# First pair's k and q through SyncE's queue in fp32, cast on VectorE; half of the first q split on GpSimd

## The chip, the cores and the metric

The kernel runs on one core of one Trainium2 chip. The metric is the device time of one execution, in microseconds; the median of the runs counts. The core has a matrix engine (TensorE, PE in the profile), VectorE (DVE), ScalarE (ACT), GpSimd (POOL) and SyncE (SP). Each has its own instruction queue and works through it in order; semaphores order them among each other. DMAs are issued from a queue: here GpSimd issues all loads, since its DMAs can cast fp32 to bf16 on the way, and SyncE issues the stores of the output.

## The reference

Sparse attention and, on its output, a soft mixture of experts. Inputs are q, k and v of shape (4, 8, 768, 64): 4 batches, 8 heads, 768 positions, 64 channels.

```python
k_min, k_max = k_chunks.min(axis=3), k_chunks.max(axis=3)      # 24 chunks of 32 keys
ub = np.sum(np.maximum(q * k_min, q * k_max), axis=-1)         # upper bound per query and chunk
ub = np.where(causal, ub, -1e9)
top_chunks = np.argsort(ub, axis=-1)[..., -6:]                 # six chunks for each query
scores = np.where(sel & causal_by_position, q @ k.T / 8, -1e9)
attn = softmax(scores) @ v
# x: attention output as (3072, 512)
logits = x @ phi                                               # 32 slots, 4 for each of 8 experts
slot_input = softmax(logits, axis=0).T @ x
slot_out[e] = relu(slot_input[e] @ w1[e]) @ w2[e]
out = softmax(logits, axis=1) @ slot_out
```

## The kernel before

The work is cut into 16 pairs of heads (4 for each batch). The two heads of a pair share the 128 partitions: 64 channels of one head above 64 of the other.

For a pair, k and q are loaded with 128 partitions of six positions each, TensorE transposes them in 12 small matmuls a tensor (`transposes`, L233), and ScalarE copies the result out of PSUM as kT and qT (`evac_T`, L242). VectorE takes the minimum and the maximum of each chunk of kT (`kmin` L251, `kmax` L257) and spreads them into a block-diagonal tile bd (L259). q is split into a negative part, min(q, 0), and a positive part, max(q, 0) (`qsplit`, L267 to L271; the positive part of the first pair is a ReLU on ScalarE, L269). Then the upper bound is the negative part times k_min plus the positive part times k_max: 12 matmuls (`ubound`, L284), on top of a causal bias (L277). VectorE finds the eight largest per query (L296) and marks the chunks below the sixth (`select`, L299); GpSimd adds one column (L298). These marks are transposed (L307, L315) and added into the score matmuls through a mask matrix smask (L325 and L335). ScalarE takes exponentials (L349), GpSimd zeroes the diagonal blocks above the diagonal (L359), TensorE multiplies with v (L377).

The order is written by hand: the engines run in the order of the program text. Before the loop stands a prologue (L170 to L616) which starts pair 0, prepares pairs 1 and 2, and fills TensorE's waits with matmuls on constants (`warm`, L224). The loop body (L618 to L720) interleaves pair i's scores with the bounds of pair i + 1, the transposes of pair i + 2 and the products with v of pair i - 1, and weaves in the expert work of a finished batch. After the loop come the experts and the output: the weights w1 and w2 of 8 experts are loaded during the whole loop, one 1 MB tile after another (`load_w`, L144), 14 into tiles of their own that are reserved from the start (w_sb), the last expert's w2 in four quarters (w_last, L150), which are used last (`last_expert_out`, L921). Output rows of 256 x 512 leave through SyncE's queue (L969, L990, L992).

At the start GpSimd issues, in this order: k and q of pair 0, k of pair 1, the select that makes the identity matrix ident (L175), q of pair 1, k and q of pairs 2 and 3, v of pair 0, four selects for the constants qgrp, caus and squad (L195 to L207), and the first weight (L211). Then comes the copy that fills the first half of smask (L213), which needs schunk from VectorE (L572).

The prologue's lines around the change:

```python
warm(8)
transposes(0, "k")
evac_T(0, "k")
kmin(0)
kmax(0)
warm(2)
transposes(0, "q")
evac_T(0, "q")
qsplit(0)
```

Of the kernel before, what the change touches and what calls it, by code (L numbers as in the profile page):

```python
# [9 lines left out]
F32 = mybir.dt.float32  # L10
# [9 lines left out]
NQT = 6  # L20
# [39 lines left out]
def kernel(  # L60
# [75 lines left out]
    def load_w(i):  # L136

        if i < E:
            src = moe_w1[i].rearrange("(a p x) f -> p a (x f)", p=P, x=2)
            dst = w_sb[i].rearrange("p (a f) -> p a f", a=NDG // 2)  # L140
        else:
            src = moe_w2[LATE[i - E]].rearrange("(a p x) d -> p a (x d)", p=P, x=4)
            dst = w_sb[i].rearrange("p (a f) -> p a f", a=NFG // 4)
        nc.gpsimd.dma_start(out=dst, in_=src)  # L144
# [8 lines left out]
    def load(i, nm, n=1):  # L153

        b, j = divmod(i, NPB)
        t = ring[nm][i // 2 % 2][:, 2 * (i % 2):2 * (i % 2 + n)]
        src = {"k": k, "q": q}[nm][b, 2 * j:2 * (j + n)]
        nc.gpsimd.dma_start(out=t, in_=src.rearrange("h (p g) d -> p h (g d)", p=P))
        for x in range(n):
            st[nm, i + x] = t[:, 2 * x:2 * x + 2]  # L160

    def load_v(i):
# [6 lines left out]

    nc.vector.memset(ones_sq, 1.0)  # L170
    nc.vector.memset(ident, 0.0)
    load(0, "k")
    load(0, "q")
    load(1, "k")
    nc.gpsimd.affine_select(  # L175
        out=ident, in_=ident, compare_op=ALU.not_equal, fill=1.0, base=0,
        pattern=[[-1, P]], channel_multiplier=1,
    )
    for t in (squad, caus, qgrp, headsel, ns_t[0], ns_t[1], c_pad):
        nc.vector.memset(t, 0.0)  # L180
    for t in v_t:
# [26 lines left out]
        out=squad, in_=squad, compare_op=ALU.not_equal, fill=-1.0, base=-NCHUNK,  # L208
        pattern=[[-CH, 2], [-64, 2], [0, NCHUNK]], channel_multiplier=1,
    )  # L210
    load_w(0)  # L211
    def spread_mask(t0, t1, copy):
        copy(  # L213
            smask[:, :, t0:t1].rearrange("p o t a x -> p o (t a) x"),
# [5 lines left out]
    def warm(n):  # L220
        r = ones_sq.rearrange("p (o c) -> p o c", o=1).broadcast_to([P, 4, P])
        for _ in range(n):
            for x in range(2):
                nc.tensor.matmul(  # L224
                    warm_ps[:, 2 * x:2 * x + 2], lhsT=ones_sq, rhs=r[:, :2], start=True, stop=True)
# [38 lines left out]
    def qsplit(i):  # L264
        qT = st["qT", i]
        t = tpu.tile([P, 2, S], BF16, name="qpn", tag="qpn")
        nc.vector.tensor_scalar_min(t[:, 0, :], qT, 0.0)  # L267
        if i == 0:
            nc.scalar.activation(t[:, 1, :], qT, func=ACT.Relu)  # L269
        else:  # L270
            nc.vector.tensor_scalar_max(t[:, 1, :], qT, 0.0)  # L271
        st["qpn", i] = t
# [45 lines left out]
    def scores(i, g):  # L318
        ps = p_sc.tile([P, 2, 512], F32, name="sc_ps", tag="sc")
        kT, qT, nsT = st["kT", i], st["qT", i], st["nsT", i]  # L320
        for kg, q0, w, c in (GROUPS_LAST if i == LAST else GROUPS)[g]:
            qs = slice(kg * P + q0, kg * P + q0 + w)
            for h in range(2):
                r = slice(h * 64, (h + 1) * 64)
                nc.tensor.matmul(  # L325
                    ps[:, h, c:c + w], lhsT=kT[r, kg * P:(kg + 1) * P], rhs=qT[r, qs],
                    start=True, stop=False,
                )
            t0, t1 = kg + q0 // P, kg + (q0 + w) // P
            runs = [(x, max(t0, x * NJ), min(t1, (x + 1) * NJ)) for x in range(2)]  # L330
            runs = [r for r in runs if r[1] < r[2]]
            for x, f, l in runs:
                for h in range(2):
                    r = slice(h * 64, (h + 1) * 64)
                    nc.tensor.matmul(  # L335
                        ps[:, h, c + (f - t0) * P:c + (l - t0) * P],
                        lhsT=smask[r, x, kg].rearrange("p a b -> p (a b)"),
                        rhs=nsT[r, (f - x * NJ) * P:(l - x * NJ) * P], start=False, stop=(l == t1),
                    )
        st["scps", i, g] = ps  # L340

    def expo(i, g, masked=True):
        pieces = (GROUPS_LAST if i == LAST else GROUPS)[g]
        w = sum(x[2] for x in pieces)
        if w == 512:
            e = ep.tile([P, 2, 512], BF16, name="e_sb", tag="e_sb")
        else:
            e = ep3.tile([P, 2, 384], BF16, name="e3_sb", tag="e3_sb")
        nc.scalar.activation(e[:, :, :w], st.pop(("scps", i, g))[:, :, :w], func=ACT.Exp, scale=scale)  # L349

        st["e", i, g] = e
        if masked:
            mask(i, g)
# [187 lines left out]
    def moe_ct_copy(b):  # L541
        nc.vector.tensor_copy(cT_all[:, b * NQT:(b + 1) * NQT, :], st.pop(("ctps", b)))


    def have(i):
        return 0 <= i < NPAIR

    def moe(step, i):

        if have(i) and i % NPB == NPB - 1:  # L550
            step(i // NPB)
# [5 lines left out]
    def weights(i):  # L557
        nonlocal nw
        for _ in range(wplan.get(i, 0)):
            load_w(nw)  # L560
            nw += 1

    warm(8)
    transposes(0, "k")
    evac_T(0, "k")
# [3 lines left out]
    transposes(0, "q")  # L569
    evac_T(0, "q")  # L570
    qsplit(0)
    nc.vector.tensor_tensor(schunk[:, :, :, 0], squad[:, :, 0, :], squad[:, :, 1, :], op=ALU.add)  # L572
    spread_mask(0, NJ, nc.gpsimd.tensor_copy)
    warm(2)
# [40 lines left out]
    kmax(2)  # L615
    qsplit(2)  # L616

    for i in range(1, NPAIR):  # L618
        slots = have(i - 3) and (i - 3) % NPB == NPB - 1
        if i >= EARLY:  # L620
            wt = ctx.enter_context(tc.tile_pool(name=f"wt{i}", bufs=1))
            if i < LAST:
                w_sb.append(wt.tile([P, NFG * Dm], BF16, name=f"w_sb{i}"))
                weights(i)
            else:
                w_last = [wt.tile([P, NFG, Dm // 2], BF16, name=f"w_last{y}") for y in range(2)]
                for y in (1, 0):
                    load_w_half(w_last[y], y)
        scores(i, 0)
        expo(i, 0)  # L630
        moe(moe_max, i - 3)
        scores(i, 1)
        expo(i, 1)
        if have(i + 1):
            ubound(i + 1)
        if i < LAST - 1:
            moe(moe_bound, i - 3)
        if have(i - 2):
            normalise(i - 2)
        if i == LAST - 1:  # L640
            moe(moe_bound, i - 3)
        if i == LAST:
            moe_ct_copy(B - 2)
        if have(i + 1):
            select(i + 1)
        moe(moe_comb, i - 3)
        if have(i + 2):
            transposes(i + 2, "k")
            evac_T(i + 2, "k")
        if not slots:  # L650
            if have(i + 2):
                load_v(i + 2)
            if i < EARLY:
                weights(i)
        if i != LAST - 1:
            pv(i - 1, [0, 1, 2])
        for g in (2, 3):
            scores(i, g)
            expo(i, g, not slots)
            if g == 2 and i == LAST - 1:  # L660
                pv(i - 1, [0, 1, 2])
            if g == 2 and i == LAST:
                x_transposes(i - 2)
        moe(moe_exp, i - 3)
        if slots:
            mask(i, 2)
            mask(i, 3)
        if have(i - 2) and i < LAST:
            x_transposes(i - 2)
        pv(i - 1, [3])  # L670
        if have(i + 2):
            transposes(i + 2, "q")
            evac_T(i + 2, "q")
            kmin(i + 2)
        if i < LAST - 1:
            moe(moe_exp2, i - 3)
        if have(i - 2):
            evac_x(i - 2)
        if have(i + 2):
            kmax(i + 2)  # L680
        if i < LAST - 1:
            moe(moe_scale, i - 3)
        if slots:
            if have(i + 2):
                load_v(i + 2)
            if i < EARLY:
                weights(i)
        scores(i, 4)
        expo(i, 4)
        if have(i + 5) and i % 2:  # L690
            load(i + 5, "k", 2)
            load(i + 5, "q", 2)
        if i == LAST - 1:
            moe(moe_exp2, i - 3)
            moe(moe_scale, i - 3)
        if i == LAST:
            pv(i - 1, [4, 5])
        moe(moe_comb2, i - 3)
        scores(i, 5)
        expo(i, 5)  # L700
        if have(i + 1):
            ns_transposes(i + 1)
            evac_ns(i + 1)
        if i < LAST:
            pv(i - 1, [4])
        moe(moe_dispatch, i - 3)
        if i < LAST:
            pv(i - 1, [5])
        if have(i + 2):
            qsplit(i + 2)  # L710
        if i < LAST - 1:
            moe(moe_ct, i - 4)
        elif i == LAST - 1:
            moe(moe_ct, i - 3)
        moe(moe_logits, i - 2)
        moe(moe_copy, i - 2)
        if i == LAST - 2:
            l_ctx.close()
        if i == LAST - 1:
            u_ctx.close()  # L720
# [304 lines left out]
```

## Time and profile before

| | |
|---|---|
| median of three runs | 159.91 us (158.8 to 159.99) |
| span of the profiled execution, first to last instruction | 156.8 us |
| its own time, taken as its span and what lies around it | 3.1 us between that span and the median |
| TensorE busy | 136.5 us (87%) |
| VectorE, ScalarE busy | 121.9 and 122.8 us (78% each) |
| GpSimd busy | 98.7 us (63%) |
| moved by GpSimd's DMA queue | 26.25 MB in 40032 packets |
| moved by the other queue, the stores | 6.29 MB in 3072 packets |
| mean granted TensorE clock | 0.982 of full speed |

The profile gives one execution. Rows of a timeline hold the start and the duration in microseconds, the engine, the line, the operation, the tile written and the tiles read, shapes, the count, and in brackets how long the engine had been idle before and what released it. PEld is a weight load of TensorE. In a window's row stand the length, then the busy time and count of PE, PEld, DVE, ACT and POOL, the granted clock, the DMA share and GB/s. Bytes are counted where they are written, so a load that casts to bf16 counts half of what it reads.

### The profile page before, as it was taken

To read this page: it belongs to the slowest core of one execution; us is meant where nothing else is said; L and a number is where in the kernel's file an instruction comes from. 1 tells how busy PE (TensorE), PEld (TensorE's weight loads), DVE (VectorE), ACT (ScalarE), POOL (GpSimd) and SP (SyncE) were. 2 spreads that over 40 slices of the span, in tenths; PEclk is the share of its full clock that TensorE was granted. 3 is DMA by queue.
4 is the path that set the end of the run, shared out by engine and by line. 5 is a ranking of instruction groups with operands and counts; after the bars stand their busy time and mean duration, and the time that the engine had idled before them with its cause. 6 is when DMAs were issued, how large, how long until landed. Compare 5 with 4: busy or idle time off the path is not lost.

```text
span 156.8 us, 5988 instructions
## 1 busy us (share of the span) xinstructions
PE 136.5 (87%) x2464; PEld 93.2 (59%) x2464; DVE 121.9 (78%) x437; ACT 122.8 (78%) x171; POOL 98.7 (63%) x192
## 2 busy tenths in 40 slices
PE   7796789999999999999999899999979999977500
PEld 4463466767766776766777677766657854633100
DVE  5478887999999998999899899999753761178720
ACT  3479899999999889999989999998789532276520
POOL 6999647958877876697597975869696810000000
PEclk9999999999999999999999999999999999999975
DMA  2999999999999999999999999999999999949995
GB/s 37 160 172 195 194 193 221 172 201 203 196 214 199 201 202 207 204 197 210 186 198 205 205 203 201 208 200 198 211 197 216 212 215 198 151 158 399 419 420 223
DMA packets 43131, 32.92 MB, mean 210 GB/s; under 512 B 26208, under 2 KB 37984, under 8 KB 43104
## 3 DMA queue, kind: packets, MB, share of 16 engines
q0 software_dynamic: 40032, 26.25, 113.9%
q1 hardware_dynamic: 3072, 6.29, 10.3%
q8 instruction: 19, 0.31, 0.7%
q14 instruction: 8, 0.07, 0.1%
HBM read 52.49 MB, written 6.29 MB: 375 GB/s over the span
## 4 chain that ended last, share of the span: by engine, by line
PE 54%; ACT 18%; DVE 12%; issue 6%; DMA 5%; POOL 1%; DVEq 0%; ACTq 0%; POOLq 0%
ACT e_sb L349 11%; PE sc_ps L325 10%; PE at_ps L377 8%; PE sc_ps L335 7%; PE tr_ps L233 5%; PE xT_ps L399 4%; ACT qT L242 4%; DMA out_dram<-o_sb 3%; DMA q_in<-in_q_dram 3%; PE ub_ps L284 2%; PE h_ps L852 2%; PE ub_ps L277 2%; DVE x_sb L390 2%; DVE o_sb L944 1%; DVE mx L296 1%
## 5 line engine op out<-in xcount | busy, mean ns | idle before, releaser
L349 ACT ACTIVATE e_sb<-sc_ps 128x1024 bf16<-128x1024 f32 (+1 forms) x96 | 83.2, 919 | 6.0 <-PE sc_ps L335 5.5
L359 POOL TENSOR_SCALAR_AFFINE_SELECT e_sb<-e_sb 128x256 bf16<-128x256 bf16 x96 | 40.2, 437 | 17.6 <-ACT e_sb L349 17.4
L325 PE MATMUL sc_ps<-qT,kT 64*128 64x384 bf16 (+3 forms) x258 | 36.8, 306 | 2.9 <-ACT e_sb L349 2.2
L335 PE MATMUL sc_ps<-nsT,smask 64*128 64x384 bf16 (+2 forms) x294 | 38.1, 284 | 0.1
L377 PE MATMUL at_ps<-v_t,e_sb 128*128 128x65 bf16 x642 | 27.7, 193 | 0.9 <-PE sc_ps L335 0.6
L377 PEld LDWEIGHTS <-e_sb 128*128 128x128 bf16 x642 | 23.6, 97 | 3.5 <-issue 1.3
L325 PEld LDWEIGHTS <-kT 64*128 64x128 bf16 x258 | 14.0, 93 | 10.9 <-issue 5.5
L296 DVE MAX8 mx<-ub_ps 128x8 f32<-128x8 f32 (+1 forms) x192 | 16.8, 162 | 3.2 <-PE ub_ps L284 3.0
L164 POOL DMA_DIRECT2D v_t<-in_v_dram x16 | 16.7, 1044 | 3.6 <-PE xT_ps L399 1.8
L251 DVE TENSOR_REDUCE mm<-kT 128x24 bf16<-128x768 bf16 x16 | 15.1, 944 | 3.0 <-ACT kT L242 2.9
L335 PEld LDWEIGHTS <-smask 64*128 64x128 bf16 x294 | 15.0, 94 | 3.6 <-issue 0.6
L390 DVE TENSOR_TENSOR x_sb<-at_ps,inv 128x768 bf16<-128x768 f32 (+1 forms) x17 | 15.5, 910 | 0.6
L242 ACT COPY kT<-tr_ps 128x768 bf16<-128x768 bf16 x16 | 12.9, 804 | 3.5 <-PE tr_ps L233 3.5
L257 DVE TENSOR_REDUCE mm<-kT 128x24 bf16<-128x768 bf16 x16 | 15.1, 943 | 0.0
L242 ACT COPY qT<-tr_ps 128x768 bf16<-128x768 bf16 x16 | 12.8, 801 | 2.4 <-PE tr_ps L233 2.4
L144 POOL DMA_DIRECT2D w_sb<-in_moe_w_dram x15 | 10.7, 712 | 0.0
L410 DVE COPY xT_sb<-xT_ps 128x768 bf16<-128x768 bf16 (+1 forms) x15 | 8.0, 536 | 1.6 <-PE xT_ps L399 1.6
L233 PE MATMUL tr_ps<-ident,q_in 128*64 128x128 bf16 x192 | 8.4, 223 | 0.7 <-DMA q_in<-in_q_dram 0.5
L233 PE MATMUL tr_ps<-ident,k_in 128*64 128x128 bf16 x192 | 8.4, 223 | 0.5 <-DMA k_in<-in_k_dram 0.5
L399 PE MATMUL xT_ps<-ident,x_sb 128*128 128x128 bf16 x96 | 8.3, 221 | 0.4 <-DVE x_sb L390 0.3
L271 DVE TENSOR_SCALAR qpn<-qT 128x768 bf16<-128x768 bf16 x15 | 8.3, 553 | 0.0
L284 PE MATMUL ub_ps<-bd,qpn 128*128 128x48 bf16 x192 | 7.6, 183 | 0.4 <-DVE qpn L267 0.4
(147 smaller groups left out, 209.7 us busy)
## 6 DMA issues: line engine op xcount, KB each, us to landing
w_sb<-in_moe_w_dram POOLq DMA_DIRECT2D x15, 1024.0 KB, 16.3
out_dram<-o_sb SPq DMA_DIRECT2D x8, 512.0 KB, 4.6
v_t<-in_v_dram POOLq DMA_DIRECT2D x16, 192.0 KB, 12.4
k_in<-in_k_dram POOLq DMA_DIRECT2D x7, 384.0 KB, 11.8
q_in<-in_q_dram POOLq DMA_DIRECT2D x7, 384.0 KB, 13.0
out_dram<-o_sb SPq DMA_DIRECT2D x8, 256.0 KB, 2.9
w_last<-in_moe_w_dram POOLq DMA_DIRECT2D x4, 256.0 KB, 19.6
k_in<-in_k_dram POOLq DMA_DIRECT2D x2, 192.0 KB, 4.1
```

The lines of the kernel that those rows point to most:

```text
L164: nc.gpsimd.dma_start(out=v_t[i % NV][:, :, :, :D], in_=v[b, 2 * j:2 * j + 2].rearrange("h (g p) d -> p h g d", p=P),)
L233: nc.tensor.matmul(ps[h * 64:(h + 1) * 64, g, :], lhsT=src[:, h, g * D:(g + 1) * D], rhs=ident, is_transpose=True,)
L242: nc.scalar.copy(t.rearrange("d (p g) -> d p g", g=NQT), st.pop((nm + "ps", i)).rearrange("d g p -> d p g"),)
L251: nc.vector.tensor_reduce(mm[:, 0, 0, :], kT, axis=AX.X, op=ALU.min)
L257: nc.vector.tensor_reduce(mm[:, 1, 0, :], kT, axis=AX.X, op=ALU.max)
L296: nc.vector.max(mx[:, a, :], ub[:, a, :max(8, 4 * t + 4)])
L325: nc.tensor.matmul(ps[:, h, c:c + w], lhsT=kT[r, kg * P:(kg + 1) * P], rhs=qT[r, qs], start=True, stop=False,)
L335: nc.tensor.matmul(ps[:, h, c + (f - t0) * P:c + (l - t0) * P], lhsT=smask[r, x, kg].rearrange("p a b -> p (a b)"), rhs=nsT[r, (f - x * NJ ...
L349: nc.scalar.activation(e[:, :, :w], st.pop(("scps", i, g))[:, :, :w], func=ACT.Exp, scale=scale)
L359: nc.gpsimd.affine_select(out=e[:, :, c:c + P], in_=e[:, :, c:c + P], compare_op=ALU.is_ge, fill=0.0, base=0, pattern=[[0, 2], [1, P]], ch ...
L377: nc.tensor.matmul(o, lhsT=st["e", i, g][:, h, c:c + P], rhs=v_t[i % NV][:, h, kg, :D + 1], start=(kg == 0), stop=(kg == t),)
L390: nc.vector.tensor_tensor(st["x", b][:, t0:t1, 2 * j:2 * j + 2, :].rearrange("p t h d -> p h t d"), at[:, :, :, :D], inv.broadcast_to([P, ...
```

## The change

The first pair's k and q are no longer loaded by GpSimd's casting DMA. SyncE issues two plain fp32 loads into a staging area, which lies in the tile of the fourteenth weight; that tile is loaded much later. VectorE casts the two into the ring buffers in which the other pairs arrive. On GpSimd, ident now comes ahead of the load of pair 1's k. The negative part of the first q moves from VectorE to GpSimd, and the first weight is asked for behind it. The loop body is rewritten: the calls of each iteration are named in four lists (for usual iterations, for those with expert work, for the last but one and the last), which a function `step` turns into calls.

```diff
-    load(0, "k")
-    load(0, "q")
-    load(1, "k")
+    stage = w_sb[EARLY - 1].bitcast(F32).rearrange("p (n h c) -> p n h c", n=2, c=512)[:, :, :, :NQT * D]
+    for n, (nm, src) in enumerate((("k", k), ("q", q))):
+        nc.sync.dma_start(out=stage[:, n], in_=src[0, :2].rearrange("h (p g) d -> p h (g d)", p=P))
     nc.gpsimd.affine_select(
         out=ident, in_=ident, compare_op=ALU.not_equal, fill=1.0, base=0,
         pattern=[[-1, P]], channel_multiplier=1,
     )
+    load(1, "k")
...
-    load_w(0)
...
-        nc.vector.tensor_scalar_min(t[:, 0, :], qT, 0.0)
+        (nc.gpsimd if i == 0 else nc.vector).tensor_scalar_min(t[:, 0, :], qT, 0.0)
...
+    def cast(n, nm):
+        t = ring[nm][0][:, :2]
+        nc.vector.tensor_copy(t, stage[:, n])
+        st[nm, 0] = t
+
+    cast(0, "k")
+    cast(1, "q")
     warm(8)
     transposes(0, "k")
...
     qsplit(0)
+    load_w(0)
     nc.vector.tensor_tensor(schunk[:, :, :, 0], squad[:, :, 0, :], squad[:, :, 1, :], op=ALU.add)
     spread_mask(0, NJ, nc.gpsimd.tensor_copy)
...
+    PLAIN = """sc:0 ex:0 mk:0 sc:1 ex:1 mk:1 ub norm sel trk evk lv lw pv:0:1:2 sc:2 ex:2 mk:2 sc:3 ex:3 mk:3
+        xt pv:3 trq evq kmin evx kmax sc:4 ex:4 mk:4 lkq sc:5 ex:5 mk:5 ns evns pv:4 pv:5 qs
+        moe_ct moe_logits moe_copy"""
...
+        order = FINAL if i == LAST else BEFORE_LAST if i == LAST - 1 else SLOTS if slots else PLAIN
+        for what in order.split():
...
+            step(i, what)
```

More of the change, by code (lines that the diff above doesn't have):

```diff
@@ L616, with step @@
     qsplit(2)
+    def step(i, what):
+        name, *arg = what.split(":")
+        arg = [int(x) for x in arg]
+        if name == "sc":
+            scores(i, arg[0])
+        elif name == "ex":
+            expo(i, arg[0], False)
+        elif name == "mk":
+            mask(i, arg[0])
+        elif name == "pv":
+            pv(i - 1, arg)
+        elif name == "norm":
+            if have(i - 2):
+                normalise(i - 2)
+        elif name == "xt":
+            if have(i - 2):
+                x_transposes(i - 2)
+        elif name == "evx":
+            if have(i - 2):
+                evac_x(i - 2)
+        elif name in ("ub", "sel", "ns", "evns"):
+            if have(i + 1):
+                {"ub": ubound, "sel": select, "ns": ns_transposes, "evns": evac_ns}[name](i + 1)
+        elif name in ("trk", "trq"):
+            if have(i + 2):
+                transposes(i + 2, name[2])
+        elif name in ("evk", "evq"):
+            if have(i + 2):
+                evac_T(i + 2, name[2])
+        elif name in ("kmin", "kmax", "qs"):
+            if have(i + 2):
+                {"kmin": kmin, "kmax": kmax, "qs": qsplit}[name](i + 2)
+        elif name == "lv":
+            if have(i + 2):
+                load_v(i + 2)
+        elif name == "lw":
+            if i < EARLY:
+                weights(i)
+        elif name == "lkq":
+            if have(i + 5) and i % 2:
+                load(i + 5, "k", 2)
+                load(i + 5, "q", 2)
+        else:
+            off = {"moe_dispatch": 3, "moe_ct": 4, "moe_logits": 2, "moe_copy": 2, "moe_ct3": 3}.get(name, 3)
+            fn = {
+                "moe_max": moe_max, "moe_bound": moe_bound, "moe_comb": moe_comb, "moe_exp": moe_exp,
+                "moe_exp2": moe_exp2, "moe_scale": moe_scale, "moe_comb2": moe_comb2, "moe_dispatch": moe_dispatch,
+                "moe_ct": moe_ct, "moe_ct3": moe_ct, "moe_logits": moe_logits, "moe_copy": moe_copy,
+                "moe_ctc": moe_ct_copy,
+            }[name]
+            moe(fn, i - off)
@@ new lines @@
+    PLAIN = """sc:0 ex:0 mk:0 sc:1 ex:1 mk:1 ub norm sel trk evk lv lw pv:0:1:2 sc:2 ex:2 mk:2 sc:3 ex:3 mk:3
+        xt pv:3 trq evq kmin evx kmax sc:4 ex:4 mk:4 lkq sc:5 ex:5 mk:5 ns evns pv:4 pv:5 qs
+        moe_ct moe_logits moe_copy"""
+    SLOTS = """sc:0 ex:0 mk:0 moe_max sc:1 ex:1 mk:1 ub moe_bound norm sel moe_comb trk evk pv:0:1:2 sc:2 ex:2 sc:3 ex:3
+        moe_exp mk:2 mk:3 xt pv:3 trq evq kmin moe_exp2 evx kmax moe_scale lv lw sc:4 ex:4 mk:4 lkq moe_comb2
+        sc:5 ex:5 mk:5 ns evns pv:4 moe_dispatch pv:5 qs moe_ct moe_logits moe_copy"""
@@ L618 @@
+    BEFORE_LAST = """sc:0 ex:0 mk:0 moe_max sc:1 ex:1 mk:1 ub norm moe_bound sel moe_comb trk evk sc:2 ex:2 pv:0:1:2
+        sc:3 ex:3 moe_exp mk:2 mk:3 xt pv:3 trq evq kmin evx kmax lv lw sc:4 ex:4 mk:4 lkq moe_exp2 moe_scale moe_comb2
+        sc:5 ex:5 mk:5 ns evns pv:4 moe_dispatch pv:5 qs moe_ct3 moe_logits moe_copy"""
+    FINAL = """sc:0 ex:0 mk:0 sc:1 ex:1 mk:1 norm pv:0:1:2 sc:2 ex:2 mk:2 xt sc:3 ex:3 mk:3
+        pv:3 evx sc:4 ex:4 mk:4 pv:4:5 sc:5 ex:5 mk:5"""
     for i in range(1, NPAIR):
@@ L628 @@
                     load_w_half(w_last[y], y)
[L629 to L716, printed above, removed]
+        order = FINAL if i == LAST else BEFORE_LAST if i == LAST - 1 else SLOTS if slots else PLAIN
@@ L717 @@
+        for what in order.split():
+            if i == LAST and what == "norm":
+                normalise(i - 2)
+                moe_ct_copy(B - 2)
+                continue
+            step(i, what)
         if i == LAST - 2:
```

## The prediction

> **What bounds the kernel now.** I read the page first, for the shares and the DMA rows, then the timeline of the first 13 us, where the change lies, then the timeline of the last 20 us, to see what a gain there would still meet.
>
> ```profile
> span 156.8 us, 5988 instructions
> ...
> DMA  2999999999999999999999999999999999949995
> ...
> q0 software_dynamic: 40032, 26.25, 113.9%
> ```
>
> No engine is the bound over the whole span, but the DMA engines are busy in nearly every slice, and nearly all of it is GpSimd's queue (q0), which casts fp32 to bf16 on the way.
>
> ```profile
> 3.00:4.00 1.00, 1.00 (x7) 0.71 (x5) 0.23 (x3) 0.00 (x0) 0.91 (x3) 1.00 1.10 145
> 4.00:5.00 1.00, 0.74 (x10) 0.32 (x10) 0.00 (x0) 0.00 (x0) 1.00 (x2) 1.00 1.26 177
> 5.00:6.00 1.00, 0.92 (x16) 0.52 (x12) 0.00 (x0) 0.58 (x1) 1.00 (x2) 1.00 1.11 111
> ...
> 137.00:138.00 1.00, 0.84 (x12) 0.41 (x9) 0.68 (x2) 0.87 (x3) 0.00 (x0) 1.00 0.42 65
> 138.00:139.00 1.00, 0.57 (x6) 0.31 (x6) 0.36 (x2) 0.27 (x1) 0.00 (x0) 1.00 0.01 1
> ```
>
> These are one-microsecond windows; the last column is GB/s. The queue starts to move bytes at about 3 us and runs dry at 138 us. In between it is one long backlog.
>
> ```profile
> 137.55 0.29 PE L921 MATMUL so_last<-w_last,hT_pad 128*32 128x256 bf16 x4
> 138.43 0.29 PE L921 MATMUL so_last<-w_last,hT_pad 128*32 128x256 bf16 x4 [0.58 <-DMA w_last<-in_moe_w_dram]
> 138.83 0.48 DVE L974 SCALAR_TENSOR_TENSOR so_all<-so_last,zinv,so_part 128x256 bf16<-128x256 f32 x1 [0.64 <-ACT o_sb L941]
> ```
>
> The end of that backlog is the last quarter of w_last, and TensorE waits for it. Without data missing, the second four L921 would have begun at 137.55 + 0.29 = 137.84 and not 138.43: compute has 0.59 us of slack there, and L974, from which most of the output hangs, follows. So the end is set by **two trains that arrive nearly together**: the compute chain from the first k and q, and the stream of GpSimd's queue. The time falls by the smaller of what the stream gains and what compute gains plus 0.59.
>
> Now the start, where both trains set off:
>
> ```profile
> 1.13 3.46 PE L224 MATMUL warm_ps<-ones_sq 128*128 128x256 bf16 x16 [1.13 <-DVE ones_sq L170]
> 1.32 0.84 POOL L158 DMA_DIRECT2D k_in<-in_k_dram  x1 [0.80 <-POOLq L1009]
> 2.15 0.73 POOL L158 DMA_DIRECT2D q_in<-in_q_dram  x1
> 2.87 0.72 POOL L158 DMA_DIRECT2D k_in<-in_k_dram  x1
> 3.69 0.31 POOL L175 TENSOR_SCALAR_AFFINE_SELECT ident<-ident 128x128 bf16<-128x128 bf16 x1
> 4.85 0.53 PE L233 MATMUL tr_ps<-ident,k_in 128*64 128x128 bf16 x12 [0.26 <-DMA k_in<-in_k_dram]
> 5.42 0.80 ACT L242 COPY kT<-tr_ps 128x768 bf16<-128x768 bf16 x1 [3.33 <-PE tr_ps L233]
> 6.25 0.95 DVE L251 TENSOR_REDUCE mm<-kT 128x24 bf16<-128x768 bf16 x1 [2.91 <-ACT kT L242]
> 6.40 0.53 PE L233 MATMUL tr_ps<-ident,q_in 128*64 128x128 bf16 x12 [0.48 <-DMA q_in<-in_q_dram]
> 6.96 0.80 ACT L242 COPY qT<-tr_ps 128x768 bf16<-128x768 bf16 x1 [0.75 <-PE tr_ps L233]
> 7.79 0.84 ACT L269 ACTIVATE qpn<-qT 128x768 bf16<-128x768 bf16 x1
> 8.10 0.26 DVE L259 TENSOR_TENSOR bd<-mm,headsel 128x96 bf16<-128x96 bf16 x1
> 8.27 0.35 DVE L267 TENSOR_SCALAR qpn<-qT 128x768 bf16<-128x768 bf16 x1
> 8.30 0.47 POOL L207 TENSOR_SCALAR_AFFINE_SELECT squad<-squad 128x96 bf16<-128x96 bf16 x1
> 8.70 0.46 PE L284 MATMUL ub_ps<-bd,qpn 128*128 128x48 bf16 x12
> 9.47 0.84 POOL L213 COPY smask<-schunk 128x768 bf16<-128x768 bf16 x1
> 12.15 4.37 ACT L349 ACTIVATE e_sb<-sc_ps 128x1024 bf16<-128x1024 f32 x5 [0.68 <-PE sc_ps L335]
> ```
>
> k lands at 4.85, q at 6.40. The upper bounds (L284, 8.70) wait for bd (8.10 + 0.26) and then for the negative half of q, L267, which stands behind it on VectorE. The first exponential comes at 12.15, and from there the loop runs with its engines full.
>
> **The change, part by part.** First, the loads on SyncE's queue. The trace has no fp32 load there; its nearest rows are the wait that starts SyncE's queue (total, times, longest) and its stores, 256 KB each in L969 and 512 KB in L992 (issue times, then landing times).
>
> ```profile
> SPq L1009 <- PEq L1009: 0.8, 1, 0.8
> ...
> L969 SPq DMA_DIRECT2D out_dram<-o_sb x6: 534/578/628, 138.0 to 141.8; - x6
> DMA to landing us min/median/max: 2.5/2.9/2.9
> ...
> L992 SPq DMA_DIRECT2D out_dram<-o_sb x8: 333/662/1120, 142.4 to 149.3; - x8
> DMA to landing us min/median/max: 3.4/4.6/5.3
> ```
>
> SyncE is free at 0.8 us. A 256 KB store landed in 2.5 us at best and a 512 KB one in 3.4; 384 KB lies half way, 2.95, so k lands near 3.8 (bounds 3.4 and, by the slowest store, 6.1). q is issued 0.6 later; the distance of the two stores makes 0.9 us for 256 KB more, 1.35 for 384 KB, so q lands near 5.2 (4.4 to 7.4).
>
> Second, two casts on VectorE, 768 fp32 elements a partition. Not in the trace; the bounds are 0.35 us (L267, bf16 to bf16) and 0.95 (L251, the same element count at one element a step). I take the middle, 0.65. They stand ahead of kmin, so **kmin also waits for q's landing**, and behind VectorE's opening memsets, which end long before 3.8.
>
> k: cast until 4.5, but TensorE has its 16 warm-up matmuls until 1.13 + 3.46 = 4.59, so the transposes begin at 4.6, 0.25 earlier than now. kT is there at 5.97, kmin starts at 6.0. q: cast 5.2 to 5.85, transposes 5.9 (0.5 earlier), qT done at 7.3, ReLU on ScalarE until 8.13. bd ends at 8.1 (0.25 earlier).
>
> Third, the negative half on GpSimd. GpSimd works without a break from 1.32 to 8.77, and two issues of 0.84 and 0.73 leave it, so its selects end at 8.77 - 1.57 = 7.2 and it is free when qT comes. The operation is not in the trace: the copy L213 of the same 768 elements took 0.84, VectorE's form 0.35, and GpSimd's two-input form gives the upper end:
>
> ```profile
> L460 POOL TENSOR_TENSOR ld<-lg,m_run 128x192 f32<-128x192 f32 x3 | 1.8, 597 | 0.0
> ```
>
> 597 ns for 192 elements is 3.1 ns each, 2.4 us for 768. I take the copy's 0.84, one input as here: 7.3 to 8.15. Behind the min on GpSimd wait the issue of the first weight and the mask copy (then 8.9 to 9.7, still ahead of 9.47 + 0.84 = 10.3 now), so moving the weight costs nothing: v and four loads stand ahead of it in the backlog. L284 can begin at about 8.2 instead of 8.70; bd, ReLU and min arrive within 0.05 us of each other. **Compute gains 0.5**, of which I keep 0.45, since behind the bounds TensorE also waits for the second pair's kT (ScalarE, 0.4 earlier).
>
> Fourth, the stream. k and q (192 KB each after the cast) leave it: by the windows they are gone at about 5.5 us (145 + 177 + half of 111, plus a little before 3 us, makes 393 KB). Afterwards the engines move 786 KB in fp32 for the same two, but from about 1 us earlier, and the second pair's k is issued behind ident alone, at 1.32 + 0.31 = 1.63 instead of 2.87. With q's last byte written half a microsecond before it lands (4.7), what follows starts 0.8 us earlier. I take **0.9 for the stream**, bounds 0 and 1.4.
>
> Fifth, the loop is rewritten as lists of steps. Read slot by slot they issue the same calls in the same order as the old body, the two last pairs included, so this costs nothing.
>
> The sum: the smaller of 0.9 and 0.45 + 0.59 = 1.04 is 0.9 at L974. Output stores of the first half-tiles move by 0.45 only, but the engines are nearly idle then (1 GB/s from 138 to 139), so I let only 0.1 be lost: 0.8 us. Span 156.8 to 156.0; the median of the runs, 159.91, lies 3.1 above the span, so **159.1 us**.
>
> **Where the Trainium skill speaks against it.** The trace shows VectorE's fast form beside GpSimd's DMA issues:
>
> ```profile
> 13.34 0.76 POOL L158 DMA_DIRECT2D q_in<-in_q_dram  x1
> 13.68 0.60 DVE L267 TENSOR_SCALAR qpn<-qT 128x768 bf16<-128x768 bf16 x1
> 14.07 0.73 POOL L144 DMA_DIRECT2D w_sb<-in_moe_w_dram  x1
> 14.20 0.78 DVE L271 TENSOR_SCALAR qpn<-qT 128x768 bf16<-128x768 bf16 x1
> ```
>
> The issues took their usual 0.73 to 0.76, and the operation that takes 0.35 at 8.27 took 0.60 and 0.78: here VectorE was held up. The Trainium skill ("SBUF — State Buffer", section "Who interferes with whom") says that a copy or cast in a two-port mode and GpSimd exclude each other for a whole instruction, whichever began first; its warning on "DVE blocks DMA" names the fp32 copy as one that keeps GpSimd from writing descriptors. By that rule GpSimd would lose the casts' time. The trace agrees that they collide, and shows so far the other loser.
>
> **The rivals.**
>
> 1. *The stream does not move.* The two loads use the same 16 engines whichever queue holds them, so what is saved in one queue is spent in the other and the end of w_last stays at 138.4. For: the DMA row is full everywhere. Against: the engines move almost nothing before 3 us. Then compute only waits longer: 0 to 0.2, 159.8 us. The Trainium skill ("DMA: Bandwidth & Descriptors", "Issuing engines are not separate DMA queues") states just this.
> 2. *The casts hold GpSimd.* Both casts fall into GpSimd's issues. If it waits out 2 x 0.65 us, its selects end at 8.5, min at 9.35, L284 starts 0.65 late; compute arrives at 137.84 + 0.65 = 138.5 against 138.43 now: no gain, 160.0 us. For: the collisions above; against: the loser in them.
> 3. *Slower: q lands late on SyncE's queue*, and both the transposes of q and kmin behind its cast go with it. If q lands at T, bd is ready 0.65 (cast) + 1.85 (both reductions, 6.25 to 8.10) + 0.26 later, and with the hand-over L284 starts at T + 2.9: equal to now at T = 5.8, and with the slack of 0.59 a loss from 6.4 on. At the slow bound, 7.4, the loss is 1.0: 160.9 us. For: 5.3 us for a store of 512 KB; against: those stores queue behind each other, these loads are first.
> 4. *More than I count*: q at 4.4 and a stream earlier by 1.4, with the slack used up: 1.4 us, 158.5.
>
> That the change doesn't do what it says is rival 1 at its end: k is ready before TensorE's warm-up lets it in, and a gain in q alone dies in the wait for w_last.
>
> **How the numbers follow.** Forecast 0.56, rival 1 0.16, rival 2 0.11, rival 3 0.09, rival 4 0.08. The three runs of before spread over 1.2 us, so about 1% (1.6 us) is what a measurement of this kernel can tell from no change. The range goes from 158.1 (rival 4, with some of the spread) to 160.5 (rival 2 and the near half of rival 3). Faster by over 1% is half of rival 4 and a tail of the forecast, 0.12; slower by over 1% the far end of rival 3, 0.07; within 1% the rest, 0.81.
>
> **What the changed profile would show.** SyncE's loads landing at 3.8 and 5.2; casts of 0.65; k's transposes at 4.6, held by the warm-up; min of 0.84 on GpSimd; L284 at 8.2 and the first exponential at 11.7; GpSimd's queue dry at 137 and no wait for w_last ahead of the last L921. I am wrong if q lands after 6.4, if the min takes over 1.2 us, or if the queue still runs dry at 138.

## The result, and the profile after

The changed kernel takes 160.25 us at the median against 159.69 us before: a ratio of 1.0042, 95% interval 1.0025 to 1.0059, or 0.4 to 0.9 us more. (The ratio is estimated from the fast runs alone and need not be the quotient of the two medians.) It was forecast 0.8 us faster. The time lies inside the range that was given, on its slow side.

The page of the changed kernel, the same rows as before:

```profile
span 158.3 us, 5991 instructions
...
DMA  5999999999999999999999999999999999459994
...
q0 software_dynamic: 39488, 25.86, 111.1%
q1 hardware_dynamic: 3616, 7.08, 11.7%
```

0.39 MB have left GpSimd's queue and 0.79 MB in fp32 have joined the other. Of the 40 slices, the first is busier on the DMA engines (5 instead of 2), and the gap near the end is two slices long (45) instead of one (4). Neither says what the loss is. The timeline of the first 13 us does:

```profile
3.80 0.56 DVE L565 CAST k_in<-w_sb 128x768 bf16<-128x768 f32 x1 [0.46 <-DMA w_sb<-in_k_dram]
...
5.49 0.58 DVE L565 CAST q_in<-w_sb 128x768 bf16<-128x768 f32 x1 [1.13 <-DMA w_sb<-in_q_dram]
6.00 0.93 DVE L251 TENSOR_REDUCE mm<-kT 128x24 bf16<-128x768 bf16 x1
6.70 0.80 ACT L242 COPY qT<-tr_ps 128x768 bf16<-128x768 bf16 x1 [0.89 <-PE tr_ps L233]
7.07 0.28 POOL L208 TENSOR_SCALAR_AFFINE_SELECT squad<-squad 128x96 bf16<-128x96 bf16 x1
7.59 2.14 POOL L267 TENSOR_SCALAR qpn<-qT 128x768 bf16<-128x768 bf16 x1 [0.24 <-ACT qT L242]
7.82 0.71 DVE L259 TENSOR_TENSOR bd<-mm,headsel 128x96 bf16<-128x96 bf16 x1
9.79 0.47 PE L284 MATMUL ub_ps<-bd,qpn 128*128 128x48 bf16 x12 [0.57 <-POOL qpn L267]
13.21 1.02 ACT L349 ACTIVATE e_sb<-sc_ps 128x1024 bf16<-128x1024 f32 x1 [0.92 <-PE sc_ps L335]
```

k lands at 3.8 and q at 5.5, the casts take 0.56 and 0.58, and q is transposed 0.3 us earlier than before. Then the min on GpSimd takes 2.14 us, from 7.59 to 9.73, and the bounds L284 wait for it: 9.79 instead of 8.70. The first exponential is 1.06 late, at 13.21.

At the other end, the wait for w_last is gone:

```profile
138.75 0.40 PE L912 MATMUL so_last<-w_last,hT_pad 128*32 128x256 bf16 x8
...
139.18 4.21 SPq L960 DMA_DIRECT2D out_dram<-o_sb  x6
139.31 0.47 DVE L965 SCALAR_TENSOR_TENSOR so_all<-so_last,zinv,so_part 128x256 bf16<-128x256 f32 x1
```

All eight matmuls (L921 before, L912 now) run in one go, 1.2 us later than the first four did. The combination of the halves (L974 before, L965 now) is only 0.48 late, but the first store is 1.2 late, and the end came 1.5 late. Before, the first store stood at

```profile
137.98 4.37 SPq L969 DMA_DIRECT2D out_dram<-o_sb  x6
```

which is ahead of the second four L921 (138.43) that waited for w_last. Part of this 1.5 is the luck of one execution; a second pair of profiles, below, shows how much.

### The profile page after: what moved, and what is told of

The parts are those of the page before. It is cut to its first block, busy times and chain, and to the rows that moved or that the text cites. A ratio compares the mean times of both kernels' runs of the same rounds, so it can differ in the third digit from the quotient of the medians.

```text
span 158.3 us, 5991 instructions
## 1 busy us (share of the span) xinstructions
PE 136.3 (86%) x2463; PEld 93.0 (59%) x2464; DVE 123.6 (78%) x438; ACT 123.1 (78%) x171; POOL 99.5 (63%) x191
## 4 chain that ended last, share of the span: by engine, by line
PE 54%; ACT 16%; DVE 11%; DMA 8%; issue 5%; POOL 1%; SPq 0%; DVEq 0%; ACTq 0%
PE sc_ps L325 10%; ACT e_sb L349 10%; PE at_ps L377 9%; PE sc_ps L335 7%; PE tr_ps L233 6%; DMA out_dram<-o_sb 5%; PE xT_ps L399 4%; ACT qT L242 4%; PE ub_ps L284 3%; DMA w_sb<-in_q_dram 3%; PE h_ps L843 2%; PE ub_ps L277 2%; ACT o_sb L932 2%; DVE x_sb L390 2%; POOL qpn L267 1%
## 5 line engine op out<-in xcount | busy, mean ns | idle before, releaser
L359 POOL TENSOR_SCALAR_AFFINE_SELECT e_sb<-e_sb 128x256 bf16<-128x256 bf16 x96 | 40.1, 435 | 17.8 <-ACT e_sb L349 17.5
L284 PE MATMUL ub_ps<-bd,qpn 128*128 128x48 bf16 x192 | 7.6, 183 | 1.0 <-POOL qpn L267 0.6
```

Of the source, the lines that this page charges most:

```text
L359: nc.gpsimd.affine_select(out=e[:, :, c:c + P], in_=e[:, :, c:c + P], compare_op=ALU.is_ge, fill=0.0, base=0, pattern=[[0, 2], [1, P]], ch ...
```

## The experiments

**Theory A**: the min on GpSimd costs 2.1 us by itself and is the whole loss; the loads gain a little. **Rival B**: the loads hurt too, since pair 1's k shares the engines with them, lands late and holds TensorE ahead of the bounds. **Rival C**: the 2.14 us come from what VectorE did beside it. Later **theory D**, on the end: it follows the first store, not L974.

**The min back on VectorE.**

```diff
-        (nc.gpsimd if i == 0 else nc.vector).tensor_scalar_min(t[:, 0, :], qT, 0.0)
+        nc.vector.tensor_scalar_min(t[:, 0, :], qT, 0.0)
```

> The changed kernel with the first pair's min back on VectorE; all else of the change stays. Theory A (the min on GpSimd is the whole loss, the loads gain): bd ends near 8.1, the min on VectorE near 8.45, the bounds L284 start at 8.5 instead of 9.79, the first exponential at 11.9 instead of 13.21, and the time is 0.4 us below before (ratio 0.997). Rival B (pair 1's k lands late, because its packets now share the engines with the fp32 loads; its transposes stand ahead of the bounds in TensorE's queue): it lands at 8.0 again, L284 follows its transposes by the 1.03 us that it did before (7.67 to 8.70), so at 9.05; first exponential 12.5, time 0.3 us above before (ratio 1.002).

159.06 us against 159.25: ratio 0.9983 (0.9962 to 1.0004). The timeline:

```profile
4.66 0.80 PE L233 MATMUL tr_ps<-ident,k_in 128*64 128x128 bf16 x12
6.92 0.53 PE L233 MATMUL tr_ps<-ident,k_in 128*64 128x128 bf16 x12
...
8.76 0.47 PE L284 MATMUL ub_ps<-bd,qpn 128*128 128x48 bf16 x12 [0.65 <-DVE qpn L267]
12.18 2.64 ACT L349 ACTIVATE e_sb<-sc_ps 128x1024 bf16<-128x1024 f32 x3 [0.91 <-PE sc_ps L335]
```

The loss is gone, so it was the min: A's 0.997 lies inside the interval, B's 1.002 outside. L284 starts at 8.76 and not at 8.5. Pair 1's k (second row) did not hold it this time; the chain does, and it begins with the warm-up (chain of the same run, in order of time):

```profile
1.13 3.59 PE warm_ps L224 x16
4.72 0.75 PE tr_ps L233 x7
...
6.33 0.95 DVE mm L251
7.29 0.87 DVE mm L257
...
8.18 0.26 DVE bd L259
8.44 0.28 DVE qpn L267
...
8.76 0.47 PE ub_ps L284 x12
```

The path is now that of k, not of q: the constant matmuls end at 4.7, then the transposes of k, and behind them VectorE's two reductions, bd and min in a row. What q gained is worth nothing here. And the 12 transposes of k took 0.80 us, where before and in the changed kernel they took 0.53: see the last section.

**Only GpSimd's part of the change, with the loads as before.**

```diff
-    load_w(0)
...
+        (nc.gpsimd if i == 0 else nc.vector).tensor_scalar_min(t[:, 0, :], qT, 0.0)
...
     qsplit(0)
+    load_w(0)
```

> The kernel before with only the GpSimd part of the change: the first pair's min on GpSimd and the first weight asked for behind it; loads as before. Theory A: GpSimd's selects end at 8.77, the min takes 2.1 us there, L284 starts at 11.0 instead of 8.70 (2.3 later); less the 0.59 us of slack at w_last the time is 1.7 us above before (ratio 1.011). Rival C (the 2.14 us came from what VectorE did beside it; alone it takes the 0.9 that the copy's row gives): L284 at 9.7, time 0.4 us above before (ratio 1.003).

160.77 us against 159.25: ratio 1.0108 (1.0069 to 1.0148), the size that A gave (1.011). That A met it so closely is luck: it took L284 to be 2.3 late and took off 0.59 of slack; L284 was 1.8 later than in the second profile of before (9.00, below), and the table below shows that there was no such slack. The min takes 2.21 us from 8.55 and the bounds follow it:

```profile
8.55 2.21 POOL L266 TENSOR_SCALAR qpn<-qT 128x768 bf16<-128x768 bf16 x1
10.81 0.47 PE L283 MATMUL ub_ps<-bd,qpn 128*128 128x48 bf16 x12 [1.68 <-POOL qpn L266]
14.23 1.02 ACT L348 ACTIVATE e_sb<-sc_ps 128x1024 bf16<-128x1024 f32 x1 [0.92 <-PE sc_ps L334]
```

This is worse than the full change, in which the loads let GpSimd and q come earlier.

**Pair 0's bounds ahead of pair 1's transposes** (on the kernel with the min on VectorE):

```diff
+    ubound(0)
     transposes(1, "k")
     evac_T(1, "k")
-    warm(2)
-    ubound(0)
-    transposes(1, "q")
-    evac_T(1, "q")
     spread_mask(NJ, NQT, nc.scalar.copy)
     select(0)
     load_v(1)
     warm(5)
+    transposes(1, "q")
+    evac_T(1, "q")
```

> As the run with the min on VectorE, and the bounds of pair 0 stand ahead of pair 1's transposes in TensorE's queue (two pairs of warm-up matmuls dropped with it, the mask copy on ScalarE earlier, pair 1's q behind the five warm-up ones). Theory A and B agree on the start: L284 at 8.5. Then select ends near 10.5 and the first exponential comes at 11.7, 0.45 earlier than before. By A the gain over the run with the min on VectorE is small, 0.2 us; by B it is 0.8 us, and the time falls 0.5 us below before (ratio 0.997).

159.21 us, ratio 0.9986 (0.9960 to 1.0012): no gain over the run with the min on VectorE. L284 started at 8.82, since min ended at 8.76, and pair 1's q, now behind the warm-up matmuls, took TensorE from 10.87 on and put off the transposes of the marks to 11.33; the first exponential came at 12.55. The order solved a wait that wasn't there in this execution and made another.

**GpSimd's prices by themselves** (six operations added where its queue is empty):

```diff
+    src = smask[:, 0].rearrange("p t a x -> p (t a x)")
+    for _ in range(2):
+        nc.gpsimd.tensor_scalar_min(scratch, src, 0.0)
+    nc.gpsimd.tensor_scalar_min(scratch[:, :S // 2], src[:, :S // 2], 0.0)
+    nc.gpsimd.tensor_copy(scratch, src)
+    nc.gpsimd.tensor_scalar_mul(scratch, src, 2.0)
+    nc.gpsimd.tensor_tensor(scratch, src, src, op=ALU.add)
```

> The kernel before with six operations of GpSimd alone added in the expert part, where its queue is empty and VectorE does little: min with a constant over 128 x 768 bf16 twice, over 128 x 384 once, copy, multiplication by a constant and an addition of two inputs over 128 x 768. Theory A: min takes 2.1 us for 768 elements and 1.1 for 384 by itself, the copy 0.84. Rival C: the min takes 0.9 in this quiet place.

```profile
130.57 4.36 POOL L846 TENSOR_SCALAR scratch<-smask 128x768 bf16<-128x768 bf16 x2
135.01 1.17 POOL L847 TENSOR_SCALAR scratch<-smask 128x384 bf16<-128x384 bf16 x1
136.24 0.83 POOL L848 COPY scratch<-smask 128x768 bf16<-128x768 bf16 x1
137.15 2.14 POOL L849 TENSOR_SCALAR scratch<-smask 128x768 bf16<-128x768 bf16 x1
139.37 1.47 POOL L850 TENSOR_TENSOR scratch<-smask 128x768 bf16<-128x768 bf16 x1
```

The min takes 2.2 us each here too, 1.17 for half the columns, and a multiplication by a constant the same 2.14. Rival C falls. The copy takes 0.83 and even an addition of two inputs only 1.47: an operation with a constant is the dearest of the three forms.

**A shorter stream** (the kernel before without one weight load):

```diff
-    load_w(1)
...
-                    rhs=w_sb[e][:, dg * F + f * 512:dg * F + (f + 1) * 512],
+                    rhs=w_sb[0 if e == 1 else e][:, dg * F + f * 512:dg * F + (f + 1) * 512],
```

> The kernel before with one 1 MB weight load left out: expert 1 reads expert 0's first weight, so its part of the output is another's. GpSimd's queue then ends about 4.9 us earlier and TensorE no longer waits for w_last; the prologue is as before. By the prediction's picture of the end (L974 carries the output) L974 comes 0.59 us earlier and the time falls by 0.5 to 0.6 (ratio 0.9965). By theory D (the stores move at one rate from the first one on, so the end follows the first half-tile that is stored and not L974) the time stays (ratio 1.000), and the last store's bytes come 16.3 us after the first one's as in every run so far.

159.06 us against 159.14: ratio 0.9987 (0.9960 to 1.0013). That is nearer to no change; by itself it leaves L974's 0.9965 just inside. The queue's last byte came at 136.4 us, 2.3 earlier than in the second profile of before (138.6) and not 4.9, but that was enough: TensorE no longer waits for w_last. The traces decide, with the next two profiles.

**The changed kernel and the one before, once more.**

> The changed kernel once more, for another phase of TensorE's clock: in the first trace it came up at about 4.2 us, earlier than in all but one of the others. If it comes later, pair 0's k transposes take 0.8 us instead of 0.53; the min on GpSimd takes 2.14 again and L284 starts between 9.7 and 10.3.

> The kernel before once more, for the same reason: its first trace had k's transposes at full clock (0.53 us) and L284 at 8.70. With a later clock L284 starts at 9.0 to 9.2 and the span is 157.3 to 157.6 instead of 156.8; from the first store's bytes to the last 16.3 us again.

The kernel before, second profile:

```profile
5.07 0.53 PE L233 MATMUL tr_ps<-ident,k_in 128*64 128x128 bf16 x12 [0.34 <-DMA k_in<-in_k_dram]
...
9.00 0.47 PE L284 MATMUL ub_ps<-bd,qpn 128*128 128x48 bf16 x12 [0.39 <-DVE qpn L267]
...
138.48 1.28 SPq L969 DMA_DIRECT2D out_dram<-o_sb  x2
139.10 0.29 PE L921 MATMUL so_last<-w_last,hT_pad 128*32 128x256 bf16 x4 [0.75 <-DMA w_last<-in_moe_w_dram]
139.50 0.48 DVE L974 SCALAR_TENSOR_TENSOR so_all<-so_last,zinv,so_part 128x256 bf16<-128x256 f32 x1 [0.81 <-ACT o_sb L941]
```

and of the changed one, second profile:

```profile
9.98 0.47 PE L284 MATMUL ub_ps<-bd,qpn 128*128 128x48 bf16 x12 [1.47 <-POOL qpn L267]
...
139.32 0.62 SPq L960 DMA_DIRECT2D out_dram<-o_sb  x1
139.45 0.48 DVE L965 SCALAR_TENSOR_TENSOR so_all<-so_last,zinv,so_part 128x256 bf16<-128x256 f32 x1
```

The changed kernel did what was expected of it (k's transposes 0.85, the min 2.14, L284 at 9.98). The kernel before gave the numbers that were expected (L284 at 9.00, span 157.3) for another reason: k's transposes ran at full speed there too (0.53), but k came 0.22 later and bd took 0.36 instead of 0.26.

The combination of the halves comes at the same time in both, 139.50 and 139.45, although one kernel waited for w_last and the other did not. Yet the spans, 157.3 and 158.3, differ by 1.03. The first stores, 138.48 and 139.32, differ by 0.84. From then on the stores are what moves: in the one-microsecond windows of before, the DMA engines reach a share of 1.0 at 141 us and hold it to 155. Over all profiles, those of the last two runs below included (starts in us; the last columns are the span less the first store, and the span less the last byte of a store, both from unrounded times):

| kernel | L284 | first exponential | first store | L974 | span | store to end | last byte to end |
|---|---|---|---|---|---|---|---|
| before | 8.70 | 12.15 | 137.98 | 138.83 | 156.8 | 18.8 | 1.24 |
| before, again | 9.00 | 12.42 | 138.48 | 139.50 | 157.3 | 18.8 | 1.25 |
| GpSimd's prices | 9.15 | 12.56 | 138.59 | 139.58 | 157.4 | 18.8 | 1.25 |
| shorter stream | 8.98 | 12.39 | 138.33 | 138.47 | 157.3 | 19.0 | 1.24 |
| GpSimd's part alone | 10.81 | 14.23 | 140.18 | 140.31 | 159.0 | 18.8 | 1.23 |
| min on VectorE | 8.76 | 12.18 | 137.97 | 138.10 | 157.3 | 19.4 | 1.61 |
| bounds first | 8.82 | 12.55 | 138.48 | 138.61 | 157.4 | 19.0 | 1.61 |
| positive half first | 8.74 | 12.14 | 137.95 | 138.08 | 157.0 | 19.1 | 1.61 |
| without filling | 8.71 | 12.16 | 138.12 | 138.92 | 157.3 | 19.2 | 1.62 |
| changed | 9.79 | 13.21 | 139.18 | 139.31 | 158.3 | 19.2 | 1.60 |
| changed, again | 9.98 | 13.40 | 139.32 | 139.45 | 158.3 | 19.0 | 1.61 |

Against the second profile of before, the shorter stream has L974 1.03 earlier and ends at the same time; GpSimd's part alone has L974 0.81 later, the first store 1.70 later, and ends 1.7 later. The first store predicts the end to 0.6 us, L974 to 1.4 (17.8 to 19.2 before the end). Theory D holds in the main: a delay of the compute chain goes through nearly whole (from the first exponential to the first store it is 125.8 to 126.1 us in every profile), and an earlier end of the weight stream is worth next to nothing.

The last column holds a cost that none of the theories had. With the loads on SyncE's queue, the span ends 1.6 us behind the last byte of a store; without them, 1.2. At the end SyncE waits for one DMA semaphore after another. From its waits for the stores in the two second profiles (total, times, longest), before:

```profile
SPq L1020 <- DMA out_dram<-o_sb: 2.3, 3, 1.1
```

and changed:

```profile
SPq L1011 <- DMA out_dram<-o_sb: 3.0, 2, 2.4
```

Nine such waits stand in a row in both kernels. In the kernel before, second profile, three of them have to wait, and the last to be met is the ninth, at 156.41. In the changed one two have to wait, and the last to be met is the third, at 157.08; the six behind it are met already and still take 0.06 us each. That makes the 0.37 us, in all six profiles with the new loads and in none of the five without; leaving it aside, the first store predicts the last byte to 0.4 us (17.3 to 17.8 later). That the two more DMAs on SyncE's queue are what turned the order of these waits is argued; no run tried it by itself.

**The positive half first**, on the kernel with the min on VectorE: in pair 0's bounds the six matmuls with ReLU's half stand ahead of the six with min's.

```diff
+        order = [(t, x) for t in range(NQT) for x in range(2)]
+        if i == 0:
+            order = [(t, x) for x in (1, 0) for t in range(NQT)]
```

> The run with the min on VectorE, and in pair 0's bounds the six matmuls of the positive half stand ahead of the six of the negative half, so that they run while VectorE still takes the min. L284 starts when bd is there, 8.5 instead of 8.76, and ends 0.25 earlier; the first exponential comes 0.2 earlier at the same phase of TensorE's clock. By theory D this goes through to the end: 0.2 below the run with the min on VectorE, 0.4 to 0.5 below before (ratio 0.997). If the end hung on w_last it would not show.

158.94 us against 159.14: ratio 0.9983 (0.9959 to 1.0006), no more than with the min on VectorE. Here pair 1's k held TensorE, as rival B has it:

```profile
7.71 0.53 PE L233 MATMUL tr_ps<-ident,k_in 128*64 128x128 bf16 x12 [0.89 <-DMA k_in<-in_k_dram]
8.01 0.26 DVE L259 TENSOR_TENSOR bd<-mm,headsel 128x96 bf16<-128x96 bf16 x1
8.17 0.61 PE L224 MATMUL warm_ps<-ones_sq 128*128 128x256 bf16 x4
8.62 0.29 PE L277 MATMUL ub_ps<-caus,qgrp 128*128 128x288 bf16 x1
8.74 0.46 PE L286 MATMUL ub_ps<-bd,qpn 128*128 128x48 bf16 x12
```

bd was ready at 8.27, but pair 1's k had landed late and its transposes and the filling matmuls behind them held TensorE until 8.62. In the first run with the min on VectorE the same transposes began at 6.92, and in the first profile of the changed kernel at 8.03: the landing of pair 1's k varies by a microsecond from one execution to the next. That the fp32 loads are what makes it late is not shown, since with the old loads these transposes began between 7.42 and 7.94.

**Without the filling matmuls ahead of the bounds**, on top of the last:

```diff
     evac_T(1, "k")
-    warm(2)
     ubound(0)
```

> The run with the positive half first, and the two pairs of warm-up matmuls (0.45 us) between pair 1's k transposes and pair 0's bounds dropped. In the run before, bd was there at 8.27, but pair 1's k landed at 7.7 and its transposes and the warm-up held TensorE until L284 at 8.74. If that is what held it, L284 now starts at 8.3 (when pair 1's k lands by 7.7), the first exponential comes 0.3 to 0.4 earlier, near 11.8, and by theory D the time falls as much: 0.6 to 0.8 us below before (ratio 0.9955). If pair 1's k was not the holder, nothing changes (0.9983).

158.94 us against 159.53: ratio 0.9973 (0.9955 to 0.9990). This is below the kernel before, by about 0.4 us and clear of noise, a little over half of what I expected. It is not shown to beat the two runs that it builds on: their 0.9983 lies inside its interval, and its first exponential came at 12.16 (theirs at 12.18 and 12.14) and not near 11.8. Pair 1's transposes began at 7.66, and now the bounds followed at once; but the ReLU's end, 8.64, became the last:

```profile
7.80 0.84 ACT L269 ACTIVATE qpn<-qT 128x768 bf16<-128x768 bf16 x1
8.12 0.30 PE L277 MATMUL ub_ps<-caus,qgrp 128*128 128x288 bf16 x1
8.23 0.26 DVE L259 TENSOR_TENSOR bd<-mm,headsel 128x96 bf16<-128x96 bf16 x1
8.71 0.47 PE L286 MATMUL ub_ps<-bd,qpn 128*128 128x48 bf16 x12 [0.29 <-ACT qpn L269]
```

## Why the prediction was wrong, point by point

**The min on GpSimd, taken at 0.84, took 2.14.** This is the step that failed, "I take the copy's 0.84, one input as here". I sized an operation with a constant by a copy because both read one tensor. The upper bound of 2.4 stood in the text, from the two-input row. That it lies so near 2.14 is luck, since two inputs at this shape took 1.47; but nothing in the text spoke for the lower end. The text named a min over 1.2 us as a thing that would make it wrong. L284 came 1.0 us later between the second profiles although the loads came earlier, and 1.0 to 1.2 later than with the min on VectorE. That is at least the whole loss. The Trainium skill ("GPSIMD Engine Reference", section 4.1) says that on GpSimd one-input operations run at roughly line rate; the runs here agree for the copy (0.83) and not for an operation with a constant: (2.14 - 1.17) / 384 makes 2.5 ns an element.

**The picture of the end failed too**: "the time falls by the smaller of what the stream gains and what compute gains plus 0.59". The wait for w_last is real, but L974 does not carry the end. The stores do, from the first half-tile on, and that one does not need the last quarter of w_last: before, it left at 137.98, ahead of the last L921. So there was no slack of 0.59 to soak up a late start, and the stream's gain went nowhere. Rivals 2 and 3 were priced too low by the same 0.59. The 0.1 that I let be lost for the first stores was the term that should have ruled.

**The end of the program** was put at nothing. SyncE's closing waits in their new order cost 0.37 us, whatever the start gains.

**The stream** did end earlier, as taken (0.9, bounds 0 and 1.4): the last byte of GpSimd's queue came at 137.3 and 137.4 instead of 138.1 and 138.6. It was right and worth nothing.

**The loads** came as predicted: k at 3.8 (predicted 3.8; its lower bound adds up to 3.3 and not 3.4, and nothing hangs on that), q at 5.5 (5.2), casts of 0.56 to 0.58 (0.65); in the second profile q came at 5.3 and its cast took 0.94. With the min left on VectorE they are worth 0.24 us at L284 against the second profile of before and 0.17% (interval from a gain of 0.38% to a loss of 0.04%), not 0.5: the sum let k's path end at 8.1, but its transposes ran slower (0.80 instead of 0.53), and min stands behind bd again. The closing waits take another 0.37 from them.

**bd**, counted at 0.26, took 0.71 beside the min (0.50 in the second profile). Where it began 0.04 us ahead of the min, in GpSimd's part alone, it took 0.26. I had no term for it; it did no harm, since min ended later still.

**Rival 1**, that the stream does not move: wrong, by the last bytes above. What was added to it, that k is ready before the warm-up lets it in, was right: with the min on VectorE k's cast ended at 4.54 and its transposes began at 4.66. **Rival 2**, the casts holding GpSimd: small. The selects ended at 7.35 instead of the predicted 7.2 (7.54 in the second profile), and GpSimd then still waited 0.24 for qT. The loser was VectorE again: q's cast of 0.94, and bd beside the min. It was slowed and not shut out, for bd ended at 8.53 and the min at 9.73. **Rival 3**, q late: it did not happen (q landed at 5.8 at the latest over the runs). **Rival 4** had its earlier stream nearly (0.8 and 1.2 against 1.4), and that was worth nothing either.

**The step from span to time** added 3.1 us. A changed run with a span of 158.3 took 160.07, so 1.7 lie around the span; the other 1.4 are the distance of a lucky first profile of before from the median. This moves no sign, but the readings of the start were taken from an execution faster than the usual one.

**In sum**, between the second profiles: L284 is 0.98 later, the first store 0.84 later, the stores themselves take 0.16 less, and the closing waits 0.36 more, which makes the span 1.03 longer. Over the runs, measured were 0.4 to 0.9. Of these the min is about 0.9 (an estimate from the ratios of the changed kernel and of the run with the min on VectorE, 1.0042 / 0.9983), and the loads, closing waits included, take off about 0.3, which by itself is not clear of noise.

## What to carry to other kernels

Size an operation on an engine by a row of the same form on that engine; where there is none, a bound that is 2.9 times the value taken is a reason to expect the worse when nothing hides the operation. Before counting slack at a late wait, ask which later work already runs without it: here the stores were the end, and what moved their first start moved the end nearly whole. Look behind the last byte too: the same waits in another order cost 0.37 us. And compare two profiles of the same kernel before reading differences of half a microsecond out of one.

## What the runs showed of the hardware that I had not expected

On GpSimd, over 768 bf16 elements a partition, a copy takes 0.83 us, an addition of two tensors 1.47 and a min or a multiplication with a constant 2.14 to 2.21.

TensorE's start is not the same from one execution to the next. The 16 warm-up matmuls took 3.46 us before and 3.59 in the run with the min on VectorE, and k's transposes behind them 0.53 and 0.80. The kernel before does it too, as the run with GpSimd's prices shows, which has its prologue. The granted clock in the profile's windows is 1.00 all this time, so that the slow phase is read from the durations alone:

```profile
5.05 0.79 PE L233 MATMUL tr_ps<-ident,k_in 128*64 128x128 bf16 x12 [0.34 <-DMA k_in<-in_k_dram]
6.33 0.53 PE L233 MATMUL tr_ps<-ident,q_in 128*64 128x128 bf16 x12
```

The full speed came after k's transposes and before q's there, and ahead of k's in the first profile of before. With the loads on SyncE's queue, k's transposes began at 4.4 to 4.7 and took longer than 0.53 in five of six profiles (0.62 to 0.85); with the old loads they began at 4.9 to 5.1 and did so in two of five. Transposing earlier thus runs into the slow phase more often, which takes back part of what earlier data gives. The Trainium skill ("TensorE: Matmul & The Clock Gate", Part 1) says that the clock is raised by a free-running activity window of about 3.4 us; that would give such a phase, and the rows here agree in kind, but no run here set the phase on purpose.
